# The gate's products in one stream of 512 columns, weights split on the vector engine, a reload in quarters and a new order of steps

## The chip, the core and the metric

The kernel runs on one core of a Trainium2 chip. The metric is device microseconds of that core; less is better. Engines are PE (matrix products), DVE (vector), ACT (scalar and activation), POOL (GpSimd) and SP, which issues most of the DMAs. Each works through its own instructions in order.

## What is computed

Three layers follow one another, all in fp32:

```
attention, 4 batches x 8 heads, 512 rows and 32 states each, width 64:
    a  = softmax(x @ state.T / 8)        xread = a @ state
    a2 = softmax(state @ x.T / 8)        sread = a2 @ x
    rows = concat(xread, sread) -> 4 * 544 = 2176 rows of 512
mixture of 8 experts: e = argmax(rows @ w_gate); the first 576 rows of
    an expert are kept; y = gate * (relu(row @ w1[e]) @ w2[e]), else 0
gated layer: out = (silu(y @ wg) * (y @ wv)) @ wo,   d_ff = 1536
```

## The kernel before

Batches of this input send all their 512 rows to one expert, and their 32 state rows to one expert. `one_expert_a_batch` builds on that, and a general path follows only where a register says that it isn't so. A matrix product in near fp32 precision is made of three products of split operands (hi and lo; `mm3`, L1464, run at L1466).

The work is cut into small steps, each a function under `@step`, named with batch b, half g or z (z = 0 the 512 rows, z = 1 the 32 state rows), block fc. An order written out by hand calls them, as `lg:1` or `up:0:3`; what an engine gets is in this order, and so is SP's queue of DMAs.

- Attention: `lx` (L1543) fetches a batch of x; `xt`, `xc` transpose it over PSUM; `sc` (L1611) makes scores, `sx` (ACT) copies them and `mx` (DVE) takes their maximum from the same PSUM bank; `tt`, `sub`, `ae`, `sn`, `an` and `ex2`, `et`, `ec`, `rs` are the two softmaxes; `rd`, `sr`, `qt`, `qc` read the states; `at`, `ah`, `al` turn the row softmax back and split it.
- Gate: the gate's matrix is folded with the states (`sg`, and `sgc` at L1586 splits it into `bsg`). `lg` (L1768) multiplies the rows' softmax with it, as 16 products with 8 or 16 moving columns each; `sl` does it for state rows. `ga`, `gb`, `gx` find the largest logit, `pq` (L1846) counts rows over partitions, `ge` writes the expert's number, `gf`, `gd`, `gp`, `gc` make gate weights. With a number known, `lu` (L1966) fetches w1 of this expert in four pieces of 512 KB, `ld` (L1979) w2 piece by piece, in eight shared buffers.
- Expert: `pj` (L1992) folds states and w1, `pa`, `pd` split it; for eight blocks `up`, `hh`, `hl`, then `wh`, `wl`, `dn`, with four PSUM banks for the result; `yt`, `yh`, `yl` (POOL) scale and split it. Batch 0 stays on the chip in `xb`; batches 1 and 2 go to DRAM (`ys`, tensor yd). `n1` to `n4` treat the narrow parts (state rows and the 64 kept rows of batch 3), gathered in `yF`.
- Gated layer, first block of 512 rows: w2l (L2191) fetches 36 pieces of weights, 64-bit words, in four buffers `raw2`; `da` (ACT, L2203), `db` (three DVE steps, L2212, L2213, L2216), `dc` (ACT, L2234) turn a piece into fp32 hi, and `dd` (POOL, L2239) makes lo; two tiles `hv` take part. `fu` (24 products), `fs`, `fm`, `fh`, `fl`, `fd` (12) compute a block fc as soon as its weights are there.
- Then, all weights on the chip, blocks of 512, 448 and 256 rows (`block`): rows of batch 1 are read back from yd into `xc` (`load_set`, L2466) in two DMAs of 1 MB, in the place that `raw2` gave up; `finish` copies results out of PSUM, and `rows_of`, `rest_rows` store them.

Of the kernel before, what the change touches and what calls it, by code (L numbers as in the profile page):

```python
# [1395 lines left out]
def one_expert_a_batch(  # L1396
# [890 lines left out]
    with tc.manual_schedule():  # L2287
        run("""
            lx:0 lx:1 st:0 stc:0 xt:0:0 xc:0:0 xc:0:2 st:1 xc:0:1 xc:0:3 stc:1 sc:0 sg:0 mx:0:0
            sx:0:0 sx:0:1 mx:0:1 tt:0:0 ex2:0:0 tt:0:1 sub:0:0 sg:1 ex2:0:1 xt:1:0 sub:0:1  # L2290
# [4 lines left out]
            et:1:1 sl:0 ec:1:1 ge:0:0 ae:1:1 rd:1 ga:0:1 lu:0:0 gb:0:1 gx:0:1 sr:1 sn:1:0 pq:0:1
            qt:1 qc:1 ge:0:1 sl:1 an:1:0 sn:1:1 lu:0:1 at:1:0 ah:1:0 ga:1:1 an:1:1 gf:0:0 gx:1:1
            at:1:1 al:1:0 gd:0:0 ah:1:1 pj:0:0 gf:0:1 ld:0:0:0 al:1:1 gd:0:1 ld:0:1:0 pa:0:0:0
            lg:1 ld:0:0:1 pa:0:0:1 pd:0:0:0 pd:0:0:1 pj:0:1 ga:1:0 gb:1:0 gx:1:0 gb:1:1 pa:0:1:0
            pq:1:0 up:0:0 pa:0:1:1 ge:1:0 gf:1:0 gp:0:0 hh:0:0 gp:0:1 gc:0:0 pd:0:1:0 gd:1:0
            gc:0:1 pd:0:1:1 n1:0:1 hl:0:0 wh:0:0 wh:0:1 wl:0:0 pq:1:1 lu:1:0 n1a:0:1 gp:1:0  # L2300
# [219 lines left out]
```

## Time and profile before

| | |
|---|---|
| three timed runs | 583.09 us median (582.48 to 584.33) |
| profiled execution | 584.99 us, span of the trace 583.3 us |
| busy share of the span | PE 94%, PE weight loads 76%, DVE 47%, ACT 33%, POOL 14% |
| mean granted clock of PE | 0.953 of 2.4 GHz |
| DMA | 72.51 MB, mean 124 GB/s |

An instruction's time in the trace runs from its start to its end; those of PE are pipelined, so that two starts are closer than one takes. A releaser behind an arrow is what ended the idle time before a row. A clock between the two levels (1.2 and 2.4 GHz) in a stretch is a mean over it.

### The profile page before, as it was taken

How to read it: one execution, taken by the hardware profiler on the slowest of the kernel's cores; microseconds unless marked ns; L12 is line 12 of the kernel's file. 1: busy time of each engine (PE TensorE's matmuls, PEld its weight loads, DVE VectorE, ACT ScalarE, POOL GpSimd, SP SyncE). 2: the span in 40 equal slices, each digit the busy share in tenths (PEclk: the TensorE clock that was granted, in tenths of full speed). 3: DMA queues.
4: the chain of work that ended last, by engine and by line, in shares of the span. 5: the costliest groups of instructions: out<-in, count | busy, mean ns of one | idle time of the engine just before them, and what ended most of it. 6: DMA issues, size and time to landing. Idle time of an engine off the chain costs nothing.

```text
span 583.3 us, 8745 instructions
## 1 busy us (share of the span) xinstructions
PE 547.0 (94%) x3418; PEld 444.0 (76%) x3418; DVE 271.9 (47%) x568; ACT 190.3 (33%) x367; POOL 81.5 (14%) x86
## 2 busy tenths in 40 slices
PE   4889999999789999999898799999999999999994
PEld 2676778886557778788676578888889888889993
DVE  1777327733863887799999311111121111122121
ACT  1643336433542553554555211111111111122111
POOL 1120001401300244334343100000000000000000
PEclk9966999899769999999999989999999999999998
DMA  7039997001796995758652630000040000001001
GB/s 146 18 119 360 280 278 264 2 1 72 242 364 197 376 338 180 253 157 261 189 178 75 231 131 0 1 0 1 0 136 9 1 0 1 1 30 34 2 1 42
DMA packets 66195, 72.51 MB, mean 124 GB/s; under 512 B 20384, under 2 KB 51872, under 8 KB 65632
## 3 DMA queue, kind: packets, MB, share of 16 engines
q1 hardware_dynamic: 62864, 70.98, 37.9%
q10 hardware_dynamic: 3280, 0.87, 0.8%
q8 instruction: 29, 0.48, 0.3%
q14 instruction: 22, 0.18, 0.1%
HBM read 62.14 MB, written 9.70 MB: 123 GB/s over the span
## 4 chain that ended last, share of the span: by engine, by line
PE 71%; DVE 10%; issue 6%; DMA 5%; POOL 4%; ACT 2%; ACTq 0%; SPq 0%; POOLq 0%; DVEq 0%
PE m L1466 45%; PE py L1466 13%; DVE hv L2213 3%; POOL w2r L2241 2%; PE m L1775 2%; PE m L1999 2%; DMA xcl<-yd 2%; PE m L2101 2%; POOL w L2241 1%; DMA yd<-y 1%; DMA xs<-in_x_dram 1%; PE m L1599 1%; PE m L1615 1%; DVE hv L2212 1%; PE py L2429 1%
## 5 line engine op out<-in xcount | busy, mean ns | idle before, releaser
L2417 DVE TENSOR_TENSOR sg<-sg,m 128x512 f32<-128x512 f32 (+2 forms) x36 | 20.8, 577 | 168.7 <-PE m L1466 168.7
L1466 PE MATMUL m<-xbh,w 128*128 128x512 f32 (+1 forms) x288 | 88.1, 377 | 0.6 <-POOL w L2241 0.6
L1466 PE MATMUL m<-xch,w 128*128 128x512 f32 (+1 forms) x288 | 74.3, 341 | 2.4 <-issue 2.4
L1466 PEld LDWEIGHTS m<-xbh,w 128*128 128x128 f32 x288 | 54.0, 188 | 8.9 <-POOL w L2241 1.0
L1466 PEld LDWEIGHTS m<-xch,w 128*128 128x128 f32 x288 | 50.9, 193 | 9.0 <-issue 2.8
L2416 ACT ACTIVATE sg<-m 128x512 f32<-128x512 f32 (+2 forms) x36 | 18.3, 509 | 112.2 <-PE m L1466 112.2
L1466 PE MATMUL m<-xbl,w 128*128 128x512 f32 (+1 forms) x144 | 54.3, 377 | 0.0
L1466 PE MATMUL m<-xcl,w 128*128 128x512 f32 (+1 forms) x144 | 49.5, 344 | 2.4 <-DMA xcl<-yd 2.4
L1474 ACT CAST hh<-sg 128x512 fp32r<-128x512 f32 (+2 forms) x36 | 19.1, 531 | 85.2 <-DVE sg L2417 85.2
L2241 POOL TENSOR_TENSOR w<-hv,w 128x512 fp32r<-128x512 f32 x26 | 36.9, 1418 | 67.6 <-ACT w L2236 67.6
L1466 PE MATMUL py<-w,hh 128*128 128x512 f32 x144 | 44.6, 391 | 0.0
L2213 DVE SCALAR_TENSOR_TENSOR hv<-raw,hv 128x512 int32<-128x512 int32 x36 | 43.4, 1205 | 1.2
L1466 PE MATMUL m<-hl,wh 128*128 128x512 f32 x96 | 38.9, 405 | 1.6 <-DVE hl L2030 1.6
L1466 PE MATMUL m<-hh,wh 128*128 128x512 f32 x96 | 39.7, 414 | 0.6 <-ACT hh L2025 0.6
L2216 DVE SCALAR_TENSOR_TENSOR hv<-hv 128x512 int32<-128x512 int32 x36 | 36.6, 1016 | 4.2 <-ACT hv L2206 0.7
L1466 PE MATMUL m<-hh,wl 128*128 128x512 f32 x96 | 38.5, 401 | 0.0
L1466 PE MATMUL m<-ah,wp 128*128 128x512 f32 x96 | 35.8, 414 | 0.0
L2206 ACT ACTIVATE hv<-raw 128x512 f32<-128x512 f32 x36 | 24.5, 680 | 31.3 <-POOL w L2241 19.4
L1466 PEld LDWEIGHTS m<-xcl,w 128*128 128x128 f32 x144 | 27.9, 194 | 6.2 <-DMA xcl<-yd 2.8
L1475 DVE TENSOR_TENSOR hl<-sg,hh 128x512 fp32r<-128x512 f32 (+2 forms) x36 | 20.9, 581 | 21.5 <-ACT hh L1474 21.5
L2042 DVE TENSOR_TENSOR wl<-rawb,wh 128x512 fp32r<-128x512 f32 x24 | 16.5, 690 | 30.1 <-ACT wh L2037 30.1
L1466 PEld LDWEIGHTS py<-w,hh 128*128 128x128 f32 x144 | 26.5, 188 | 4.9
(215 smaller groups left out, 974.9 us busy)
## 6 DMA issues: line engine op xcount, KB each, us to landing
rawa<-in_moe_w_dram SPq DMA_DIRECT2D x32, 512.0 KB, 6.4
rawb<-in_moe_w_dram SPq DMA_DIRECT2D x32, 512.0 KB, 7.4
raw<-in_moe_w_gate_dram SPq DMA_DIRECT2D x12, 512.0 KB, 6.0
raw<-in_moe_w_val_dram SPq DMA_DIRECT2D x12, 512.0 KB, 4.5
raw<-in_moe_w_out_dram SPq DMA_DIRECT2D x12, 512.0 KB, 4.7
yd<-y SPq DMA_DIRECT2D x8, 512.0 KB, 3.4
xs<-in_x_dram SPq DMA_DIRECT2D x14, 256.0 KB, 5.9
out_dram<-ot SPq DMA_DIRECT2D x11, 256.0 KB, 5.5
```

The source lines that it names most:

```text
L1466: nc.tensor.matmul(po, lh[a], rh[b], start=first and n == 0, stop=last_ and n == 2, tile_position=at)
L1474: nc.scalar.copy(hi, src)
L1475: nc.vector.tensor_tensor(lo, src, hi.bitcast(F32), op=ALU.subtract)
L1775: nc.tensor.matmul(po[:, c, 0:w].rearrange("p j e -> p (j e)"), v[b][part][g][:, s], bsg[:, 2 * b + g, 0:w].rearrange("p j e -> p (j e)"), ...
L1999: nc.tensor.matmul(pw[g][NS * k:NS * (k + 1), 256 * i:256 * (i + 1)], sT[r, b, NS * k:NS * (k + 1)], raws[b, 0][1][2 * h + i][r, k], start ...
L2042: nc.vector.tensor_tensor(w[1], raws[b, 0][2][fc // 2][:, fc % 2], w[0].bitcast(F32), op=ALU.subtract)
L2206: nc.scalar.activation(t[:, 0], Wn[fc, m][0][:, :, 1].bitcast(F32), AF.Copy, scale=2.0 ** -112)
L2213: nc.vector.scalar_tensor_tensor(vi, r[:, :, 0], 29, vi, op0=ALU.logical_shift_right, op1=ALU.bitwise_or)
L2216: nc.vector.scalar_tensor_tensor(vi, hw.bitcast(I32), 3, vi, op0=ALU.logical_shift_left, op1=ALU.bitwise_or)
L2241: nc.gpsimd.tensor_tensor(lo, Wn[fc, m][1][:, 1], hi.bitcast(F32), op=ALU.subtract)
L2416: nc.scalar.activation(sg, ph[0][:, 0:n], AF.Silu)
L2417: nc.vector.tensor_tensor(sg, sg, ph[1][:, 0:n], op=ALU.mult)
```

## The change

The softmax's rows are now the moving operand of `lg`: the folded gate's products, all four batches side by side in 128 columns, are held, and four products of 512 columns give logits, hi and lo part, by row of a [128, 512] bank. ACT copies it (`lc`), and four small fp32 products (`lt`) with `add2`, which picks a batch and adds its hi and lo rows, turn it back. `dd` moves from POOL to DVE. The rows of batch 1 come back through four DMAs of 512 KB into `raw2` buffers (`xc2`), from within the first block. `gF` has the tail ahead of the state rows, so that the last stores are four instead of six, and the last bank is copied in two halves. All of the order is new.

```
-    bsg = ctile([P, B * 2, 2, E], "bsg", F32R)
+    GQ = P // B
+    bsg = [ctile([P, B, GQ], "bsg%d" % g, F32R) for g in range(2)]
+    add2 = ctile([P, B, E], "add2")
+    for t in bsg:
+        nc.gpsimd.memset(t.bitcast(F32), 0.0)
...
     def sgc(g):
-        hi, lo = bsg[:, g::2, 0], bsg[:, g::2, 1]
+        hi, lo = bsg[g][:, :, 0:E], bsg[g][:, :, E:2 * E]
...
+        if g == 0:
+            i4 = ident.rearrange("p (b q) -> p b q", b=B)
+            nc.vector.tensor_tensor(add2, i4[:, :, 0:E], i4[:, :, E:2 * E], op=ALU.add)
...
     def lg(b):
-        v[b]["lg"] = po = bank([P, NC, 2, E], b == 0)
+        v[b]["lgs"] = po = bank([P, S], b == 0)
+        todo = [(g, part) for g in range(2) for part in ("hi", "lo")]
+        for g, part in todo:
+            nc.tensor.matmul(
+                po, bsg[g].rearrange("p b q -> p (b q)"), v[b][part][g],
+                start=(g, part) == todo[0], stop=(g, part) == todo[-1],
+            )
+    def lc(b):
+        v[b]["lgr"] = r = wk.tile([P, S], F32, tag="lgr", name="lgr")
+        nc.scalar.copy(r, v[b]["lgs"])
+    def lt(b):
+        v[b]["lg"] = po = bank([P, NC, E], b == 0)
         for c in range(NC):
-            s = slice(c * P, (c + 1) * P)
-            for n, (part, g) in enumerate((("hi", 0), ("lo", 0), ("lo", 1), ("hi", 1))):
-                w = 2 if part == "hi" else 1
-                nc.tensor.matmul(
-                    po[:, c, 0:w].rearrange("p j e -> p (j e)"), v[b][part][g][:, s],
-                    bsg[:, 2 * b + g, 0:w].rearrange("p j e -> p (j e)"),
-                    start=n == 0, stop=n == 3,
-                )
+            nc.tensor.matmul(
+                po[:, c], v[b]["lgr"][:, c * P:(c + 1) * P], add2[:, b], start=True, stop=True
+            )
...
     def ga(b, z):
-            src = small(z, "lsum")
-            nc.vector.tensor_reduce(
-                src, v[b]["lg"].rearrange("p c j e -> p c e j"), axis=AX.X, op=ALU.add
-            )
+        src = v[b]["pl" if z else "lg"]
...
     def dd(fc, m):
-        nc.gpsimd.tensor_tensor(lo, Wn[fc, m][1][:, 1], hi.bitcast(F32), op=ALU.subtract)
+        nc.vector.tensor_tensor(lo, Wn[fc, m][1][:, 1], hi.bitcast(F32), op=ALU.subtract)
...
+    def xc2(k):
+        t = raw2.tile([P, 2, 512], F32R, tag="raw", name="xc")
+        xc.append(t)
+        nc.sync.dma_start(t.bitcast(F32), yd[0, :, :, 512 * k:512 * (k + 1)])
...
     def finish(py, n, stores):
+            elif n < 512 and not half and j == len(py) - 1:
+                nc.scalar.copy(o[:, 0:256], p[:, 0:256])
+                nc.vector.tensor_copy(o[:, 256:DM], p[:, 256:DM])
...
     def rest_rows(j, t):
             nc.sync.dma_start(o[NC - 1, 64:P], t[0:64])
-            nc.scalar.dma_start(s_rows(0), t[64:64 + NS])
-            nc.scalar.dma_start(s_rows(1), t[64 + NS:P])
+            nc.scalar.dma_start(out[last * SEQ:last * SEQ + TAIL], t[64:P])
         else:
-            nc.sync.dma_start(out[last * SEQ:last * SEQ + TAIL], t[64:P])
-            nc.scalar.dma_start(s_rows(2), t[0:NS])
-            nc.sync.dma_start(s_rows(3), t[NS:64])
+            o = out.rearrange("(b s) d -> b s d", b=B)[:, S:SEQ]
+            for b in range(0, B, 2):
+                (nc.scalar if b else nc.sync).dma_start(o[b:b + 2], t[NS * b:NS * (b + 2)])
...
-    load_set(1, yd[0], 512)
     finish(fv["py"], S, rows_of(0))
```

Of the order, the places that matter here (each list is one engine-wide order; steps between are left out at "..."):

```
 first scores
- xc:0:1 xc:0:3 stc:1 sc:0 sg:0 mx:0:0 sx:0:0 sx:0:1 mx:0:1 tt:0:0
+ xc:0:1 xc:0:3 xt:1:2 stc:1 sc:0 sg:1 sx:0:0 mx:0:1 sx:0:1 mx:0:0 ex2:0:1 tt:0:1
 first expert
- lg:0 ex2:1:0 ... rd:0 ga:0:0 gb:0:0 ... pq:0:0 qc:0 ... ge:0:0 ... lu:0:0
+ rd:0 xc:1:1 ae:0:0 at:0:1 lx:2 ... lg:0 ... lc:0 ... lt:0 ... xt:2:0 ec:1:1 ga:0:0 xt:2:1 gb:0:0 ae:1:0 rd:1
+ xc:2:0 xc:2:1 gb:0:1 pq:0:0 ... ge:0:0 pq:0:1 ... lu:0:0
- pj:0:0 ... lg:1 ... pj:0:1 ga:1:0 ... up:0:0
+ pj:0:0 ... pj:0:1 ... lg:1 ... sl:1 lc:1 lt:1 ga:1:1 up:0:0 ... up:0:1
 batch 2 and the end of expert 0
+ pj:1:1 ... at:2:1 ... at:2:0 ... dn:0:6 ... lg:2 wh:1:0 lx:3 ... up:1:0 lc:2 rd:2 ... ld:0:1:3 ... lt:2 ... dn:0:7
+ ga:2:0 gb:2:0 gx:2:0 pq:2:0 ... n3:0:1 yt:0:0 yt:0:1 ... yt:0:2 ... dn:1:0 ... n1:1:1 ... lu:2:0
 batch 3
- dn:1:7 n1:1:1 yt:1:0 ... sc:3 ... tt:3:0 ... at:3:0 ... pj:2:0 ... lg:3 ... pj:2:1 ... up:2:0 ... dn:2:0
+ sc:3 ... dn:1:2 sx:3:0 mx:3:0 ... tt:3:1 ... up:1:3 ... up:1:4 ... pj:2:0 ... dn:1:3 ... at:3:1 ... pj:2:1 ...
+ al:3:0 ... dn:1:7 ... tx wh:2:0 yt:1:1 lg:3 ... up:2:0 ... lc:3 up:2:1 ... lt:3 ... yt:1:3 ... dn:2:0
 opening of the decoding buffers
- ... wh:2:2 gf:3:1 verdict up:2:1 ... up:2:2 gc:3:1 | ... w2l:0:0
+ ... wh:2:4 n2:2:1 dn:2:3 gc:3:1 | wl:2:4 n2a:2:1 w2l:0:0
 a block of weights
- da:4:1 w2l:5:1 dc:4:0 db:4:1 dd:4:0 n2:3:1 fd:2 n2a:3:1 da:4:2 fm:3 w2l:5:2 dc:4:1 db:4:2 fh:3 dd:4:1
+ db:4:0 da:4:1 db:4:1 w2l:5:1 dc:4:0 fu:3:1 dd:4:0 w2l:5:2 dc:4:1 ld:3:1:0 fl:2 ld:3:1:1 dd:4:1 fs:3
 its end
- da:11:2 fu:11:0 fm:10 dc:11:1 db:11:2 fh:10 dd:11:1 fu:11:1 fl:10 dc:11:2 fs:11 dd:11:2 fd:10
+ db:11:1 da:11:2 fd:9 fm:10 xc2:2 dc:11:1 db:11:2 fh:10 fu:11:0 dd:11:1 xc2:3 dc:11:2 fl:10 dd:11:2
+ fu:11:1 fs:11 fd:10 fm:11 fh:11 fl:11 fd:11
```

## Rows read from the trace of the kernel before

**Rows 1.** The page's first part: busy us, share of the span, instructions.

```profile
PE 547.0 (94%) x3418; PEld 444.0 (76%) x3418; DVE 271.9 (47%) x568; ACT 190.3 (33%) x367; POOL 81.5 (14%) x86
```

**Rows 2.** Busy time by stretches: length, engines (instructions), granted clock, DMA share, GB/s.

```profile
40.00:60.00 20.00, 19.05 (x146) 12.71 (x147) 14.51 (x65) 7.36 (x17) 3.87 (x6) 0.66 1.05 349
60.00:140.00 80.00, 79.93 (x561) 64.07 (x559) 39.09 (x82) 33.53 (x65) 8.43 (x8) 0.98 0.47 143
140.00:160.00 20.00, 16.18 (x231) 9.96 (x234) 14.62 (x44) 9.92 (x26) 7.17 (x7) 0.82 0.67 221
160.00:180.00 20.00, 17.82 (x146) 12.18 (x146) 11.09 (x50) 8.06 (x19) 0.28 (x1) 0.67 0.81 282
...
200.00:240.00 40.00, 40.00 (x220) 30.63 (x222) 30.61 (x48) 18.95 (x34) 16.07 (x11) 1.00 0.80 278
...
260.00:280.00 20.00, 18.59 (x85) 15.02 (x82) 19.17 (x25) 10.12 (x18) 9.88 (x7) 1.00 0.84 256
280.00:300.00 20.00, 18.55 (x80) 14.38 (x78) 19.07 (x24) 10.11 (x16) 8.33 (x7) 1.00 0.58 178
300.00:320.00 20.00, 18.11 (x75) 13.75 (x76) 19.17 (x24) 10.59 (x18) 8.41 (x7) 1.00 0.37 107
```

**Rows 3.** The chain that ended last: start us, us, what.

```profile
113.01 27.32 PE m L1466 x120
```

**Rows 4.** Timeline from 0 to 37 us, and one stretch by its busy times (columns as in rows 2).

```profile
14.27 1.96 PE L1615 MATMUL m<-xt,f_sT 64*32 64x512 f32 x16
...
17.71 1.97 PE L1638 MATMUL m<-f_ident,stt 128*128 128x128 f32 x8 [1.07 <-ACT stt L1625]
...
31.08 1.94 PE L1704 MATMUL m<-xs,e2t 128*32 128x64 f32 x64
...
36.93 8.18 SPq L1973 DMA_DIRECT2D rawa<-in_moe_w_dram  x8
...
16.00:17.00 1.00, 0.64 (x40) 0.54 (x28) 0.65 (x1) 0.00 (x0) 0.00 (x0) 1.00 0.06 11
```

**Rows 5.** Timeline at 17 us: copies of the first scores.

```profile
17.07 1.07 ACT L1625 COPY stt<-m 128x512 f32<-128x512 f32 x2 [4.83 <-DVE mx L1630]
```

**Rows 6.** Timeline: the counts' product, and the gate's products of batch 3.

```profile
34.92 0.45 PE L1848 MATMUL m<-f_cc,f_ones 128*128 128x16 f32 x2
...
163.40 3.58 PE L1775 MATMUL m<-f_bsg,part 128*128 128x16 f32 x16
```

**Rows 7.** Decoding: groups by shape; L2212 in one stretch; timeline from 262 us.

```profile
L2213 DVE SCALAR_TENSOR_TENSOR hv<-raw,hv 128x512 int32<-128x512 int32 x36 | 43.4, 1205 | 1.2
L2216 DVE SCALAR_TENSOR_TENSOR hv<-hv 128x512 int32<-128x512 int32 x36 | 36.6, 1016 | 4.2 <-ACT hv L2206 0.7
...
300.00:320.00 20.00, 2.51 (x6) 1.00 0.37 107
...
262.51 1.33 POOL L2241 TENSOR_TENSOR w<-hv,w 128x512 fp32r<-128x512 f32 x1 [1.30 <-ACT w L2236]
262.73 1.67 DVE L2213 SCALAR_TENSOR_TENSOR hv<-raw,hv 128x512 int32<-128x512 int32 x1
264.50 0.69 DVE L2216 SCALAR_TENSOR_TENSOR hv<-hv 128x512 int32<-128x512 int32 x1
```

**Rows 8.** Timeline of PE around the reload of batch 1's rows.

```profile
329.73 0.39 PE L1466 MATMUL m<-w2y,hl 128*128 128x512 f32 x1
332.48 1.15 PE L1466 MATMUL m<-xch,w 128*128 128x512 f32 x4 [2.36 <-issue]
336.04 0.80 PE L1466 MATMUL m<-xcl,w 128*128 128x512 f32 x1 [2.41 <-DMA xcl<-yd]
...
340.75 0.40 PE L1466 MATMUL m<-xcl,w 128*128 128x512 f32 x1
```

**Rows 9.** Timeline of the end: last copy and last store.

```profile
575.23 0.69 DVE L2397 COPY ot<-py 128x512 f32<-128x512 f32 x1 [1.38 <-PE py L1466]
...
576.75 0.57 SPq L2464 DMA_DIRECT2D out_dram<-ot  x1
```

More of the change, by code (lines that the diff above doesn't have):

```diff
@@ L2279, in fd @@
             mm3(fv["py"][j], [a[:, c] for a in h], W2[fc, 2], fc == 0, fc == NF - 1)
+    xc = []
+    @step
+    def xc2(k):
+        t = raw2.tile([P, 2, 512], F32R, tag="raw", name="xc")
+        xc.append(t)
+        nc.sync.dma_start(t.bitcast(F32), yd[0, :, :, 512 * k:512 * (k + 1)])
     def run(text):
@@ L2295, in one_expert_a_batch @@
[L2295 to L2300, printed above, removed]
@@ new lines, in one_expert_a_batch @@
+            dn:0:0 gf:1:0 gf:1:1 gd:1:0 hl:0:1 gd:1:1 gp:1:0 ld:1:0:0 wh:0:2 up:0:2 lu:0:1
+            gc:1:0 wl:0:2 sc:2 hh:0:2 hl:0:2 gp:1:1 dn:0:1 sx:2:0 mx:2:1 sx:2:1 mx:2:0 ex2:2:1
+            gc:1:1 ex2:2:0 up:0:3 wh:0:3 rs:2 wl:0:3 pj:1:0 hh:0:3 hl:0:3 tt:2:1 ld:0:1:0
+            pa:1:0:0 tt:2:0 ld:0:1:1 pa:1:0:1 sub:2:1 dn:0:2 ld:0:0:3 pd:1:0:0 ae:2:1 pd:1:0:1
+            sn:2:1 up:0:4 wh:0:4 wl:0:4 an:2:1 n1:0:1 hh:0:4 sub:2:0 hl:0:4 ae:2:0 dn:0:3
+            n1a:0:1 sn:2:0 an:2:0 up:0:5 wh:0:5 wl:0:5 n2:0:1 hh:0:5 et:2:1 n2a:0:1 dn:0:4
@@ new lines, in one_expert_a_batch @@
+            ae:3:0 pj:2:0 hl:1:3 hh:1:4 sn:3:1 dn:1:3 pa:2:0:0 pa:2:0:1 hl:1:4 an:3:1 sn:3:0
+            up:1:5 wh:1:5 pd:2:0:1 an:3:0 wl:1:5 dn:1:4 hh:1:5 pd:2:0:0 hl:1:5 up:1:6 wh:1:6
+            wl:1:6 dn:1:5 hh:1:6 hl:1:6 up:1:7 wh:1:7 wl:1:7 n3:1:1 hh:1:7 hl:1:7 at:3:1 lu:2:1
+            n3a:1:1 pj:2:1 axa:1 axv:1 ah:3:1 at:3:0 pa:2:1:1 al:3:1 dn:1:6 ah:3:0 axv:0
+            pd:2:1:1 axa:0 pa:2:1:0 ld:2:1:0 al:3:0 ld:2:0:2 pd:2:1:0 ld:2:1:1 dn:1:7 wh:2:1
+            ld:2:1:2 ld:2:1:3 wl:2:1 tx wh:2:0 yt:1:1 lg:3 txc yt:1:0 yh:1:1 up:2:0 wl:2:0
@@ new lines, in one_expert_a_batch @@
+            yh:1:0 yl:1:1 lc:3 up:2:1 hh:2:0 yl:1:0 yt:1:2 hl:2:0 lt:3 hh:2:1 ys:1:0 yt:1:3
+            n4:1:1 et:3:1 ys:1:1 ga:3:0 dn:2:0 gb:3:0 gx:3:0 ec:3:1 hl:2:1 n4v:1:1 yh:1:2 pq:3:0
+            yh:1:3 rd:3 yl:1:2 ge:3:0 n4a:1:1 gf:3:0 dn:2:1 yl:1:3 sr:3 ys:1:2 n4l:1:1 gd:3:0
+            ys:1:3 gp:3:0 wh:2:2 qt:3 up:2:2 gc:3:0 wl:2:2 qc:3 wh:2:3 sl:3 hh:2:2 wl:2:3 up:2:3
+            ga:3:1 gb:3:1 gx:3:1 silu n1:2:1 hl:2:2 hh:2:3 hl:2:3 pq:3:1 n1a:2:1 dn:2:2 ge:3:1
+            gf:3:1 verdict gd:3:1 gp:3:1 wh:2:4 n2:2:1 dn:2:3 gc:3:1
@@ L2351, in one_expert_a_batch @@
+            fs:0 db:1:2 da:2:0 n1:3:0 yt:2:0 w2l:3:0 dc:1:2 yt:2:1 ld:3:0:3 yh:2:0 db:2:0 yh:2:1
+            yl:2:0 yl:2:1 fu:0:1 n1a:3:0 yt:2:2 w2l:3:1 dc:2:0 yv:2:0 yt:2:3 yv:2:1 dd:1:2
+            n2:3:0 fm:0 da:2:1 fu:1:0 dd:2:0 n2a:3:0 fh:0 db:2:1 da:2:2 n3:3:0 db:2:2 w2l:3:2
+            dc:2:1 ys:2:0 ys:2:1 dd:2:1 fl:0 da:3:0 fu:1:1 fs:1 db:3:0 yh:2:3 yh:2:2 yl:2:3
+            n3a:3:0 yl:2:2 yv:2:3 n4:3:0 fd:0 fm:1 n4v:3:0 fh:1 yv:2:2 ys:2:2 n4a:3:0 fl:1
+            ys:2:3
         """)
@@ L2380, in one_expert_a_batch @@
     tc.no_sync_barrier()
-    exr.close()
-    xtc = ctx.enter_context(tc.tile_pool(name="f_xtc", bufs=1, side="right"))
-    sets = [xb, [xtc.tile([P, KD, 512], F32R, name="xc" + c) for c in "hl"]]
+    sets = [[[a[:, k] for k in range(KD)] for a in xb], [[a[:, q] for a in xc] for q in range(2)]]
     def finish(py, n, stores):
@@ L2452, in rest_rows @@
     def rest_rows(j, t):
-        def s_rows(b):
-            return out[b * SEQ + S:(b + 1) * SEQ]
         if j == 0:
@@ L2458, in rest_rows @@
             nc.sync.dma_start(o[NC - 1, 64:P], t[0:64])
-            nc.scalar.dma_start(s_rows(0), t[64:64 + NS])
-            nc.scalar.dma_start(s_rows(1), t[64 + NS:P])
-        else:
-            nc.sync.dma_start(out[last * SEQ:last * SEQ + TAIL], t[64:P])
-            nc.scalar.dma_start(s_rows(2), t[0:NS])
-            nc.sync.dma_start(s_rows(3), t[NS:64])
+            nc.scalar.dma_start(out[last * SEQ:last * SEQ + TAIL], t[64:P])
+        else:
+            o = out.rearrange("(b s) d -> b s d", b=B)[:, S:SEQ]
+            for b in range(0, B, 2):
+                (nc.scalar if b else nc.sync).dma_start(o[b:b + 2], t[NS * b:NS * (b + 2)])
     def load_set(i, src, n):
+        if i:
+            for k in range(KD):
+                nc.sync.dma_start(
+                    xc[k].bitcast(F32)[:, :, 0:n],
+                    src.rearrange("p q (k n) -> p k q n", k=KD)[:, k, :, 0:n],
+                )
+            return
         for q in range(2):
             nc.sync.dma_start(
-                sets[i][q].bitcast(F32)[:, :, 0:n],
+                xb[q].bitcast(F32)[:, :, 0:n],
                 src[:, q].rearrange("p (k n) -> p k n", k=KD)[:, :, 0:n],
             )
-    load_set(1, yd[0], 512)
     finish(fv["py"], S, rows_of(0))
```

135 lines of the change are left out of this document (58 added, 77 removed).

## The prediction

> **What bounds the kernel now.** The page comes first: the matmul engine (PE) is busy for 94% of the span [rows 1], so time can only go where PE waits, or where it works at a low clock. The table by stretches says where that is [rows 2]. From 60 to 140 us and from 200 to 240 us PE has nearly no gap at a granted clock of 0.98 to 1.00; that is PE's own work, and the change takes next to none of it away. Back to back, 120 products of 512 columns took 27.32 us, 0.228 us each [rows 3]; that is the 2.4 GHz level, and at 1.2 GHz the same product takes twice as long.
>
> Four places lose time. In 40 to 60 us the clock is 0.66. In 140 to 180 us PE is idle for 3.82 and 2.18 us, and the means of 0.82 and 0.67 lie between the two levels: 20 x 0.18 + 20 x 0.33 = 10.2 us of full-speed work were not done; together 16.2 us [rows 2]. From 260 to 320 us the clock is full, yet PE is idle for 1.41 + 1.45 + 1.89 = 4.75 us while the vector engine (DVE) is busy for 57.4 of 60 us: there DVE, which decodes the gated layer's weights, is the bound [rows 2]. Around 330 us PE stands still for a reload.
>
> The profiled run took 584.99 us, of which 583.3 are its span; the median of the three timed runs is 583.09. I add the terms to 584.99 and take the 1.90 us of difference off at the end.
>
> **The first 60 us: +4.7 us here, -1.7 later.** The new list puts the transposes of batch 1 (xt:1:2) ahead of the first scores (sc:0). PE works in order, so sc:0, which began at 14.27 us [rows 4], now waits for the whole of batch 1's x, which the same queue brings last; its data come in until a little after 16 us (the DMA engines' share is down to 0.06 in 16 to 17 us) [rows 4]. Four transposes more, and sc:0 starts near 16.8 us: +2.5. Against it, sx:0:0 now stands beside mx:0:1: in the trace the ACT copy waited for the DVE maximum over the same bank [rows 5], and with the swap each engine has its own: -0.7. Further on pq:0:0, whose counts choose the first expert, stands on PE behind xt:2:0, xt:2:1 and rd:1. Eight transposes took 1.97 us here [rows 4], rd took 1.94 [rows 4]; of these 3.9 us the ten small DVE steps of ga and gb cover some 2 us: +2. The x of batch 2 is now fetched ahead of the first expert's weights; were it late, pq:0:0 would wait for it too: +0.9 as an estimate, between 0 and 3. Sum +4.7: the weights' fetch, at 36.93 us before [rows 4], leaves nearer 41.5. The bounds are 0 and +8, the lower one if everything is covered. The eight transposes are then missing from the dense stretch later, about 1.7 us with what waits for them.
>
> **The gate's products (lg, lc, lt): 0.** Before, 16 products took 3.58 us [rows 6] at the low clock. Now four of 512 columns take 4 x 0.228 at the full level and 1.8 us at the low one; lc, a copy of 128x512 on ACT, is half of the 1.07 us pair in the trace [rows 5], 0.53. The four turning products in fp32 are bounded by the counts' product pq, one such product in two instructions: 0.45 us at the low clock [rows 6], so up to 1.8 us, and 0.6 if they pipeline. I take 1.2, since four in a row share fill and drain. That is 3.5 against 3.58; the small reduction over two halves goes as well. With four batches the bounds are -4 and +3 us, most of it under other work. The two memsets on POOL and the sum add2 on DVE stand ahead of everything that waits; if that cover went, they would cost under 1 us. The narrow columns moved in gF cost nothing.
>
> **Batches 2 and 3 inside the experts: -12 us.** Before, scores, softmax and gate of batch 3 stood after the last down-projection of expert 1, with nothing else for PE; that is the stretch of 140 to 180 us. In the new list sc:3 to al:3 lie among up:1:3 to dn:1:7, and pj:2 (expert 2's folded weights) is done before expert 1 ends, so lg:3 and lt:3 are followed by up:2:0, up:2:1 and dn:2:0. The 16.2 us lose their cause. I leave 4.2 us of them: dn:1:0 needs all four yt of expert 0, which on DVE stand among the gate's small steps of batch 2; n3:0:1 needs a weight piece behind the 1 MB of lx:3 on SP's queue; and the four yt of expert 1 alternate with POOL over two buffers ahead of dn:2:0. SP's ld and lu are issued in the list's new order; lu:2:0 stands behind n1:1:1, which frees its buffers, and has dn:1:2, up:1:3 and up:1:4 as cover before pj:2:0, 24 products or 5.5 us. Bounds: -16.2 and -6.
>
> **The weights' split on DVE: -3.6 us.** A weight costs DVE three steps (db) today; the middle and last take 1.205 and 1.016 us on average, where a step of that shape without POOL beside it takes 0.69 [rows 7]. In single rows: a POOL split started at 262.51 and ran 1.33 us; the DVE step at 262.73 took 1.67 us, the next one, after POOL's end, 0.69 [rows 7]. So POOL's split holds DVE up. With dd on DVE a weight gains 0.515 + 0.326 and pays 0.69: -0.15 us; six weights fall into 20 us [rows 7], so 24 into the dense 80 us: -3.6, at most the 4.75 us that PE is idle. DVE is still the bound: the three weights of a block cost 3 x (0.42 + 3 x 0.69) + 2 x 0.69 = 8.9 us, PE's 36 products 8.2. Decoding starts later in PE's work than before (after dn:2:3, not up:2:2: some 8 us less to hide behind); I charge nothing, since DVE had 9.4 us idle in 200 to 240 us [rows 2]; without that cover it would be +4. So the bounds are -4.75 and +4.
>
> By the Trainium skill ("Perfetto Trace Analysis", Optimizing Scalar/DVE Operations) GpSimd and the vector engine share a read port, so moving work between the two might not help. By that this term would be 0 and the forecast 3.6 us later; the rows above say that the step of DVE gets back more than it pays, and they decide.
>
> **The reload in quarters: -6.9 us.** PE's last product of block one starts at 329.73 us; the next four start at 332.48, then PE waits 2.41 us for xcl<-yd, restarts at the low clock and is back at full level about 340.75 us [rows 8]. Those 11 us hold 15 products, 3.4 us at full level: 7.4 us lost. The loads could leave only at 325 us, once all decoding buffers were free. Now each quarter goes into one decoding buffer as it falls free, the fourth after db:11:2. PE then still has fu:11:1, fd:10 and fd:11, 36 products or 8.2 us, against some 5 us for 512 KB. I leave 0.5 us. Bounds -7.4 and -3, if the fourth is late.
>
> **The last rows: -0.5 us.** The last copy ended at 575.92 us, and the last of six stores was issued at 576.75, behind others of its queue [rows 9]; with four stores, one of each queue left after the copy, that is about 576.2. The copy of the last bank (0.69 us [rows 9]) is cut into halves on ACT and DVE, which would save another 0.3 us if they ran side by side. The Trainium skill ("PSUM — Partial Sum Buffer", PSUM bank collisions) keeps two engines off one bank at once; by it the halves run in turn and save nothing. The row agrees: ACT's copy waited for DVE on one bank [rows 5]. Bounds -1 and +0.3.
>
> **Sum.** 4.7 - 1.7 + 0 - 12 - 3.6 - 6.9 - 0.5 = -20.0; 584.99 - 20.0 = 565.0 us for a profiled run, 563.1 against the median. I forecast 563.
>
> **Rivals.** First, *half the middle stays* and the start is worse: PE in order only moves its waits from 140 us to dn:1:0, dn:2:0 and the first experts. It keeps 8 instead of 4.2 us, the start costs 8 instead of 4.7, DVE gives nothing: 563 + 3.8 + 3.3 + 3.6 = 574. For it speaks that the clock is low through 40 to 60 us, where any delay costs double; against it the dense 60 to 140 us, where batch 2 is already mixed in without loss. Chance 0.18.
>
> Second, *more comes out*: the start costs nothing net, the whole 16.2 us go, PE never waits for DVE: 563 - 3 - 4.2 - 1.2 = 555. Chance 0.13.
>
> Third, *the quarters don't do what they say*: the last one waits behind DVE's splits, and PE stands as long as before: 563 + 6.9 = 570. Chance 0.05.
>
> Fourth, **slower**: the split in DVE's queue waits for ACT's cast of the same weight, with only two decoding tiles to work on. If the long steps stay at 1.205 and 1.016 us and each split adds 0.69 and a cast's wait of 0.6 us, a weight costs 1.3 us more than today's 3.3; over 24 weights that is +31 where I count -3.6: 563 + 3.6 + 31 = 598. It decides once a weight takes 0.7 us more than today (16.4 us of other gains over 24 weights). Against it: the new list puts another weight's db, fm or fl between a cast and its split, and the long steps go with POOL's. Chance 0.06.
>
> **How the numbers follow.** My forecast has 0.58, the rivals 0.18, 0.13, 0.05 and 0.06. The predicted time is that of the likeliest. The range of 552 to 576 takes in the two rivals that are faster, the 574 and the ends of the large terms, and leaves out the slower case. A change of 0.3%, 1.7 us, is about what a measurement of this kernel can tell from none. Only the fourth rival ends above; a sum of bad bounds could land at no change. So faster 0.92, same 0.02, slower 0.06.
>
> **What would show it.** Right: PE's gap at the reload is gone and 1.00 stands through that slice; 140 to 180 us have no low clock; POOL is nearly idle after the experts, and L2213 and L2216 of before have a mean of 0.69 us; PE's first folded product (pj) starts later than 43 us. Wrong: long steps of DVE without POOL; gaps before each DVE split; a low clock after 60 us; a fourth quarter that lands after PE's last fd.

## The result, and the profile after

The changed kernel takes 565.58 us (median of four runs, 564.59 to 566.53), the kernel before, run beside it, 582.79; the ratio is 0.971 with an interval of 0.966 to 0.975. The forecast was 563.0 in a range of 552 to 576. The profiled execution takes 566.21 us with a span of 564.6, at a mean granted clock of 0.981.

The first part of the page, and the table by stretches (length, then busy time of PE, weight loads, DVE, ACT and POOL, then clock, DMA share, GB/s), of the changed kernel:

```profile
PE 528.6 (94%) x3402; PEld 430.4 (76%) x3402; DVE 263.3 (47%) x601; ACT 193.2 (34%) x372; POOL 31.7 (6%) x52
```

```profile
40.00:60.00 20.00, 14.23 (x112) 9.82 (x112) 11.94 (x47) 7.16 (x16) 2.82 (x4) 0.74 0.53 184
60.00:140.00 80.00, 78.79 (x643) 58.77 (x643) 48.99 (x135) 38.01 (x78) 12.62 (x12) 1.00 0.77 242
140.00:160.00 20.00, 20.00 (x181) 15.65 (x179) 10.92 (x19) 9.85 (x21) 2.55 (x2) 1.00 0.55 184
160.00:180.00 20.00, 20.00 (x182) 14.89 (x181) 11.99 (x52) 8.57 (x22) 3.05 (x4) 1.00 0.38 133
200.00:240.00 40.00, 36.99 (x219) 27.05 (x217) 29.77 (x55) 17.63 (x31) 5.53 (x4) 1.00 0.82 255
260.00:280.00 20.00, 20.00 (x145) 16.37 (x144) 19.01 (x35) 11.43 (x20) 0.00 (x0) 1.00 0.71 228
280.00:300.00 20.00, 20.00 (x90) 16.57 (x89) 18.93 (x34) 12.08 (x20) 0.00 (x0) 1.00 0.67 211
300.00:320.00 20.00, 20.00 (x90) 16.58 (x89) 8.76 (x14) 5.08 (x9) 0.00 (x0) 1.00 0.64 219
```

Against [rows 2], 140 to 180 us are now full at the full clock, and so are 260 to 320 us. New is a loss of 3.0 us between 200 and 240 us, where there was none; and 40 to 60 us are no better: PE is idle for 5.77 us there at a mean clock of 0.74, where it was idle for 0.95 us at 0.66.

The reload, in the timeline of PE (against [rows 8]): the second block follows 0.22 us behind the last fd and runs on at full clock.

```profile
313.48 0.39 PE L1466 MATMUL m<-w2y,hl 128*128 128x512 f32 x1
313.70 11.04 PE L1466 MATMUL m<-xc,w 128*128 128x512 f32 x48
```

The end, in the timeline: last product, copies, last issues (against [rows 9]).

```profile
551.14 0.40 PE L1466 MATMUL py<-w2y,hl 128*128 128x512 f32 x1
551.49 0.56 ACTq L2481 DMA_DIRECT2D out_dram<-ot  x1
552.10 0.37 ACT L2418 COPY ot<-py 128x256 f32<-128x256 f32 x1 [0.64 <-PE py L1466]
552.50 0.42 DVE L2419 COPY ot<-py 128x256 f32<-128x256 f32 x1 [2.33 <-ACT ot L2418]
552.96 0.63 SPq L2485 DMA_DIRECT2D out_dram<-ot  x1
552.96 1.34 ACTq L2485 DMA_DIRECT2D out_dram<-ot  x1
```

PE's last product moved from 574.80 to 551.14 us, by 23.7. The end of the span moved by only 18.8 us: from the last product to the end there were 8.5 us, and now there are 13.4.

To compare the two orders, in which work changes its place, I count every PE instruction of a stretch at the pitch that its shape has in dense rows at full clock (0.2275 us for a product of 512 columns, 0.11 us for one of 8 or 16), and call what is left of the stretch lost. This is an estimate.

| | forecast us | lost time, after less before |
|---|---|---|
| first 60 us, net of the 1.7 us that come back later | +3.0 | +1.4 |
| 60 to 180 us, batches 2 and 3 | -12 | -14.3 |
| 180 to 320 us, decoding | -3.6 | -3.4 |
| reload | -6.9 | -7.3 |
| behind PE's last product | -0.5 | +4.9 |
| PE's own work (gate's products) | 0 | 0 |
| sum | -20.0 | -18.7 |

The first row is no larger than the scatter: five kernels that are the same up to 60 us (they are named in the last section) lie between -1.3 and +2.2 us by this count.

### The profile page after: what moved, and what is told of

The parts are those of the page before. It is cut to its first block, busy times and chain, and to the rows that moved or that the text cites. A ratio compares the mean times of both kernels' runs of the same rounds, so it can differ in the third digit from the quotient of the medians.

```text
span 564.6 us, 8671 instructions
## 1 busy us (share of the span) xinstructions
PE 528.6 (94%) x3402; PEld 430.4 (76%) x3402; DVE 263.3 (47%) x601; ACT 193.2 (34%) x372; POOL 31.7 (6%) x52
## 4 chain that ended last, share of the span: by engine, by line
PE 80%; DVE 7%; DMA 5%; ACT 2%; issue 1%; SPq 1%; POOL 1%; ACTq 1%; POOLq 0%; DVEq 0%
PE m L1466 57%; PE py L1466 13%; DMA rawb<-in_moe_w_dram 2%; DVE hv L2227 1%; DMA yd<-y 1%; DMA f_wgt<-in_moe_w_gate_dram 1%; PE m L2151 1%; PE m L2115 1%; PE py L2453 1%; PE m L1624 1%; DMA rawa<-in_moe_w_dram 1%; DVE hv L2230 1%; DMA xs<-in_x_dram 1%; DVE w L2255 1%; DVE t L2071 1%
## 5 line engine op out<-in xcount | busy, mean ns | idle before, releaser
L1466 PE MATMUL m<-xc,w 128*128 128x512 f32 (+1 forms) x432 | 77.4, 336 | 0.0
L1466 PEld LDWEIGHTS m<-xc,w 128*128 128x128 f32 x432 | 67.5, 190 | 9.1
L2440 ACT ACTIVATE sg<-m 128x512 f32<-128x512 f32 (+2 forms) x36 | 18.3, 508 | 104.4 <-PE m L1466 104.4
L1474 ACT CAST hh<-sg 128x512 fp32r<-128x512 f32 (+2 forms) x36 | 19.1, 531 | 85.7 <-DVE sg L2441 85.7
L1466 PE MATMUL m<-hl,wh 128*128 128x512 f32 x96 | 37.5, 391 | 0.0
L1466 PEld LDWEIGHTS m<-xbl,w 128*128 128x128 f32 x144 | 27.1, 188 | 3.9
L1466 PE MATMUL py<-w,hl 128*128 128x512 f32 x72 | 28.1, 390 | 0.0
L2230 DVE SCALAR_TENSOR_TENSOR hv<-hv 128x512 int32<-128x512 int32 x36 | 25.8, 717 | 3.7
L2227 DVE SCALAR_TENSOR_TENSOR hv<-raw,hv 128x512 int32<-128x512 int32 x36 | 25.9, 719 | 1.2
L2250 ACT CAST w<-hv 128x512 fp32r<-128x512 f32 x26 | 16.1, 622 | 27.8 <-DVE hv L2230 22.0
```

The lines of the kernel that those rows point to most:

```text
L1466: nc.tensor.matmul(po, lh[a], rh[b], start=first and n == 0, stop=last_ and n == 2, tile_position=at)
L1474: nc.scalar.copy(hi, src)
L2227: nc.vector.scalar_tensor_tensor(vi, r[:, :, 0], 29, vi, op0=ALU.logical_shift_right, op1=ALU.bitwise_or)
L2230: nc.vector.scalar_tensor_tensor(vi, hw.bitcast(I32), 3, vi, op0=ALU.logical_shift_left, op1=ALU.bitwise_or)
L2250: nc.scalar.copy(t[:, 0], Wn[fc, m][1][:, 1])
L2440: nc.scalar.activation(sg, ph[0][:, 0:n], AF.Silu)
```

## The experiments

Each kernel is the changed one with the edit shown. The kernel before ran beside each set of four; its medians there were 581.64, 582.60 and 584.16 us, so that between sets 1 to 2 us mean little. Where that is so, the place in the trace decides.

**Stores by batch.**

```
-            for b in range(0, B, 2):
-                (nc.scalar if b else nc.sync).dma_start(o[b:b + 2], t[NS * b:NS * (b + 2)])
+            for b in range(B):
+                (nc.scalar if b % 2 else nc.sync).dma_start(o[b], t[NS * b:NS * (b + 1)])
```

> The changed kernel, but its last bank leaves in four stores of one batch (32 rows) each, two on each queue, instead of two stores of two batches each. Theory: a store over two batches is cut so that few of the DMA engines get its packets, and that is the 4.9 us by which the stretch from PE's last product to the end of the span grew (8.5 us before, 13.4 after). Then about 565.6 - 4.9 + 0.3 = 561.0 us, and the last packets land within some 2.5 us of the last issue. Rival: the copy in two halves, or the new order of the narrow columns, is what made the end longer; then 565 to 566 us, packets still thin after 554 us.

Measured: 563.56 us (ratio to before 0.967, 0.958 to 0.975). From the last product (554.20) to the end (span 562.6) are 8.4 us: the 5.0 us are back. The median shows only 2.0 of them; its profiled run lost time elsewhere, in 40 to 60 us (see the last section) and, 4.8 us by the count above, in 220 to 240 us, where the changed kernel lost 1.1. The DMA view of the end, from 548 to 564.5 us of the changed kernel (busy share of the engines in tenths by 40 slices, GB/s by the same slices, then packets, then the issues):

```profile
DMA  0000000010078801112212111110110000000000
GB/s 0 0 0 0 0 0 0 0 40 0 0 154 179 323 5 25 30 10 70 70 35 60 30 45 45 50 65 35 45 50 35 25 25 25 0 0 0 0 0 0
DMA packets 300, 0.61 MB, mean 37 GB/s; under 512 B 36, under 2 KB 36, under 8 KB 292
out_dram<-ot SPq DMA_DIRECT2D x2, 128.0 KB
out_dram<-ot ACTq DMA_DIRECT2D x2, 128.0 KB, 2.9
```

and from 551 to 562.5 us with stores by batch:

```profile
DMA  0000000000010000498949995000100001000000
DMA packets 360, 0.61 MB, mean 53 GB/s; under 512 B 96, under 2 KB 96, under 8 KB 352
out_dram<-ot SPq DMA_DIRECT2D x1, 128.0 KB
out_dram<-ot ACTq DMA_DIRECT2D x1, 128.0 KB, 2.9
out_dram<-ot SPq DMA_DIRECT2D x2, 64.0 KB
out_dram<-ot ACTq DMA_DIRECT2D x2, 64.0 KB
```

The bytes are the same. With stores by batch they leave mostly at 8 or 9 tenths of the engines; over two batches at 2 tenths or less, for nearly 8 us by the GB/s row. The packets under 512 B (4 bytes each) tell how a store was shared out: six stores have 96 of them, 16 each; the four stores of the changed kernel have 36, which is 2 x 16 for the first two and 2 for each of those over two batches. So, by this count, each of these ran on two of sixteen engines.

The Trainium skill says this ("DMA: Bandwidth & Descriptors", Why a DMA increments its semaphore by 16 and not by 1): a DMA is shared over the largest number of engines, up to 16, that divides the slowest dimension of both its sides. Here these are 64 partitions and 2 batches, which gives 2, and the trace agrees with its 36 packets.

**Undivided last copy.**

```
-            elif n < 512 and not half and j == len(py) - 1:
-                nc.scalar.copy(o[:, 0:256], p[:, 0:256])
-                nc.vector.tensor_copy(o[:, 256:DM], p[:, 256:DM])
```

> The changed kernel with its last bank copied whole by DVE, as before the change; the stores over two batches stay. If the stores are what is slow: 565.6 us within 0.5 (one copy of about 0.69 us for two halves of 0.37 and 0.42 us in turn). If the halves are the cause of the long end: 561. If the halves did save their 0.3 us somewhere: 565.9.

Measured: 564.88 us (0.972, 0.965 to 0.980). Just outside the first case: the end is 12.2 us instead of 13.4. In the timeline, with the last product at 547.95:

```profile
548.38 0.69 DVE L2418 COPY ot<-py 128x512 f32<-128x512 f32 x1 [1.40 <-PE py L1466]
549.10 0.63 SPq L2482 DMA_DIRECT2D out_dram<-ot  x1
```

The stores are issued 1.15 us behind the last product; with halves it was 1.82 (551.14 to 552.96). The halves cost 0.67 us for two reasons that the rows of the changed kernel show: they run in turn (552.10, 552.50), and ACT's half begins only when ACT's queue is done with issuing a store (551.49 + 0.56). The rest of the 1.2 us by which the end is shorter is not explained.

**Both edits of the end.**

> The changed kernel with both edits of its end: stores by batch, and the last bank copied whole by DVE. From PE's last product to the end of the span: 13.41 us in the changed kernel, 8.39 with the stores by batch alone, 12.23 with the undivided copy alone. If both effects are what the traces say, they add: 7.2 us, and 565.6 - 6.2 = 559.4 us. Rival: the undivided copy's 1.2 us is a matter of when the stores meet, and adds nothing here: 560.6. If neither holds and the ends only differed by chance: 564 to 566.

Measured: 561.15 us (0.964, 0.960 to 0.968). In the trace the end is 8.5 us (549.73 to 558.20), no shorter than with the stores alone. By this trace the rival holds, and the copy's gain does not add in the span. It is not settled: the two later kernels with the same end ("four edits together" and the last one) have 7.9 and 8.0 us there, so that up to 0.5 us of it may remain. The median is 4.4 us below the changed kernel's, of the 4.9 by which the end had grown.

**The split back on POOL.**

```
-        nc.vector.tensor_tensor(lo, Wn[fc, m][1][:, 1], hi.bitcast(F32), op=ALU.subtract)
+        nc.gpsimd.tensor_tensor(lo, Wn[fc, m][1][:, 1], hi.bitcast(F32), op=ALU.subtract)
```

> The changed kernel with one line back: the weights' lo part (dd) is computed on POOL again, in the new order. The forecast's step: the two long DVE steps of the decoding go from 0.72 us back toward 1.2 and 1.0, DVE is the bound from 240 to 310 us again, and the time is 565.6 + 3.6 = 569.2 us (567.5 to 571). Rival, that moving work between the two engines changes nothing here: 565.6 within 0.6. Second rival, that the new order leans on DVE's split (two decoding tiles, split late behind POOL): over 572.

Measured: 574.08 us (0.988, 0.980 to 0.995), 8.5 more; in the trace PE ends 5.4 us later. Groups of the page (number, busy us, mean ns), of the changed kernel and of this one:

```profile
L2230 DVE SCALAR_TENSOR_TENSOR hv<-hv 128x512 int32<-128x512 int32 x36 | 25.8, 717 | 3.7
L2227 DVE SCALAR_TENSOR_TENSOR hv<-raw,hv 128x512 int32<-128x512 int32 x36 | 25.9, 719 | 1.2
```

```profile
L2255 POOL TENSOR_TENSOR w<-hv,w 128x512 fp32r<-128x512 f32 x26 | 36.8, 1418 | 57.7 <-ACT w L2250 48.9
L2227 DVE SCALAR_TENSOR_TENSOR hv<-raw,hv 128x512 int32<-128x512 int32 x36 | 39.6, 1099 | 1.2
L2230 DVE SCALAR_TENSOR_TENSOR hv<-hv 128x512 int32<-128x512 int32 x36 | 36.4, 1010 | 3.9 <-ACT hv L2220 0.4
```

One line changes the two long steps by 0.38 and 0.29 us each, and in the same rows the split itself takes 1.42 us on POOL. The second rival, over 572 us, holds. By the trace, from the first fu to the last fd, the decoding takes 124.0 us instead of 117.7. In the new order DVE's split is worth more than the 3.6 us that I gave it against the old one. How much of this is the long steps and how much the late split with only two decoding tiles, this edit does not separate.

**The reload at once.** xc2 is taken out of the list; behind the decoding its buffers are given up, and two loads of 1 MB go into a tile of their own.

```
-        ... xc2:0 ... xc2:1 ... xc2:2 ... xc2:3
+    exr.close()
+    xtc = ctx.enter_context(tc.tile_pool(name="f_xtc", bufs=1, side="right"))
...
+    load_set(1, yd[0], 512)
     finish(fv["py"], S, rows_of(0))
```

> The changed kernel, but the rows of batch 1 come back as before the change: two loads of 1 MB into a tile of their own, in the place that the decoding buffers give up when all of them are free. Forecast's step: PE stands still and falls to the low clock between the last fd and the second block, 565.6 + 7 = 572.5 us (571 to 573.5). Rival: as the new list ends its decoding earlier, some 10 us before the last product, the two loads are hidden as well and the quarters are worth 0 to 2 us: 565.6 to 567.5.

Measured: 573.78 us (0.986, 0.979 to 0.994), 8.2 more. The gap of before stands there again, after a last fd at 314.00:

```profile
316.53 1.17 PE L1466 MATMUL m<-xch,w 128*128 128x512 f32 x4 [2.14 <-issue]
320.41 0.80 PE L1466 MATMUL m<-xcl,w 128*128 128x512 f32 x1 [2.71 <-DMA xcl<-yd]
```

From the last fd to the first output product of the second block are 19.1 us instead of 11.1. Decoding ended early here too: the last step that reads one of its buffers ran from 302.91 to 303.60 us. Yet the two loads were issued at 309.55 and 309.92 us, behind a load of the next rows (xbh) on SP's queue:

```profile
308.98 0.34 SPq L2493 DMA_DIRECT2D xbh<-yd  x1
309.55 0.33 SPq L2493 DMA_DIRECT2D xch<-yd  x1
```

That one overwrites what fu:11:1 still reads, whose last product starts at 308.56 us, so it could not leave before.

**Batch 3 behind expert 1.** The steps from sc:3 to al:3:0 move out of the blocks of expert 1 to right behind dn:1:7.

```
- ... dn:1:2 sx:3:0 mx:3:0 ... dn:1:6 ah:3:0 ... dn:1:7 wh:2:1
+ ... dn:1:7 sc:3 sx:3:0 mx:3:0 ... ah:3:0 axv:0 axa:0 al:3:0 wh:2:1
```

> The changed kernel, with the scores and both softmaxes of batch 3, from sc:3 to al:3, moved out of expert 1 to right behind its last down-projection (dn:1:7), in the same order. Expert 2's folded weights stay early. If the largest term of the forecast has the right cause (PE had nothing else while batch 3's softmax ran), PE stands and its clock falls between expert 1 and expert 2 again: 10 to 16 us lost, 576 to 582 us. Rival: it was the early folding of expert 2 and the spread over DVE, ACT and POOL that mattered, and the chain of batch 3 is covered by the rest: 565.6 to 569.

Measured: 581.35 us (0.997, 0.993 to 1.000): 15.8 more, all but the whole gain of the change. The stretches show the old picture, a PE without work and then a low clock:

```profile
140.00:160.00 20.00, 15.90 (x169) 11.49 (x167) 7.99 (x18) 7.01 (x14) 0.00 (x0) 1.00 0.54 186
160.00:180.00 20.00, 14.72 (x122) 11.32 (x123) 13.26 (x35) 9.88 (x23) 7.48 (x6) 0.74 0.17 62
```

So the early fold of expert 2 (kept here) does not bring the gain by itself; the place of batch 3's softmax does. Whether that place would bring it without the early fold was not tried.

**Scores first.**

```
- xc:0:1 xc:0:3 xt:1:2 stc:1 sc:0 sg:1
+ xc:0:1 xc:0:3 stc:1 sc:0 xt:1:2 sg:1
```

> The changed kernel, with the transposes of batch 1 (xt:1:2) behind the first scores again. In the changed kernel sc:0 starts at 16.00 us, after the last piece of x; here it should start at 14.3 as before the change. If this is on the path to the first weights, as the forecast's first term says, the fetch (lu:0:0, at 38.79) leaves some 1.5 us earlier and the time is about 564. Rival: the xt put off takes its place a few us later, on a PE and an ACT that are both busy, and the fetch leaves within 0.5 us of 38.8; then 565.6 within 1.

Measured: 563.35 us (0.968, 0.961 to 0.975), 2.2 less. sc:0 starts at 13.40, the counts pq:0:0 come at 33.55 instead of 36.86, the fetch leaves at 35.56 instead of 38.87, and dn:0:0 starts 2.1 us earlier.

**Fold before casts.**

```
- pd:0:0:0 wh:0:0 pd:0:0:1 wh:0:1 wl:0:0 wl:0:1 lg:1 pa:0:1:1 pa:0:1:0 pd:0:1:1 pd:0:1:0 sl:1 lc:1 lt:1
+ pd:0:0:0 pd:0:0:1 lg:1 pa:0:1:1 pa:0:1:0 pd:0:1:1 pd:0:1:0 sl:1 lc:1 wh:0:0 wh:0:1 wl:0:0 wl:0:1 lt:1
```

> The changed kernel, with the casts and splits of the first two w2 pieces (wh:0:0, wh:0:1, wl:0:0, wl:0:1) behind those of expert 0's second folded half (pa:0:1, pd:0:1) and the copy lc:1. In the changed kernel PE stands idle from 49.6 to 52.4 us: ACT's wh:0:0 waits for a w2 piece until 49.7, and pa:0:1 and lc:1, whose inputs lie ready at 48.2 and 49.3, are queued behind it; lt:1 and up:0:0 wait for them. Theory: up:0:0 starts near 52 instead of 54.1, and the time falls by 2 us, to 563.5 (562.5 to 564.5). Rival: the casts are then late for dn:0:0 (60.53), and it starts where it did: 565.6 within 1.

Measured: 565.42 us (0.972, 0.964 to 0.980): no change. The wait in the changed kernel, in ACT's timeline (three rows) and PE's:

```profile
49.71 1.14 ACT L2051 CAST wh<-rawb 128x512 fp32r<-128x512 f32 x2 [3.04 <-DMA rawb<-in_moe_w_dram]
50.75 1.06 ACT L2022 CAST wp<-m 128x512 fp32r<-128x512 f32 x2
51.71 0.60 ACT L1790 COPY lgr<-m 128x512 f32<-128x512 f32 x1
...
52.40 1.85 PE L1797 MATMUL m<-f_add,lgr 128*128 128x8 f32 x8 [2.75 <-ACT lgr L1790]
```

PE's wait before lt:1 went from 2.75 us to 0.20, as the theory said; but in this execution PE was at the low clock from 45 to 51 us (0.50, where the changed kernel shows 0.98), and up:0:0 started at 54.49 instead of 54.10. So what the wait itself is worth is not shown here.

**Stores of batch 2 first.**

```
- w2l:3:2 dc:2:1 ys:2:0 ys:2:1 dd:2:1
+ ys:2:0 ys:2:1 w2l:3:2 dc:2:1 dd:2:1
```

> The changed kernel, with the stores of batch 2's first two row groups (ys:2:0, ys:2:1) ahead of the weight piece w2l:3:2 on SP's queue instead of behind it. In the changed kernel PE waits from 217.6 to 220.6 us: ACT's yh:2:3 waits for these stores to free a buffer, n3a:3:0 is queued behind it on ACT, and PE's n4:3:0 waits for that. The rows were ready at 206 us, but SP stood at w2l:3:2, whose buffer came free at 211.05, and issued the stores at 211.48. Theory: the stores leave at 206, PE's gap of 3 us is gone, and the time falls by 2.5 to 4 us, to 562.5. Rival: DVE sets the pace of the decoding from there on, and what PE doesn't wait for here it waits for by 260 us: 565 to 566.

Measured: 563.20 us (0.967, 0.960 to 0.975), 2.4 less. The wait in the changed kernel, one row each of SP's, ACT's and PE's timeline:

```profile
211.48 1.19 SPq L2090 DMA_DIRECT2D yd<-y  x2
218.13 0.62 ACT L2081 CAST y<-t 128x512 fp32r<-128x512 f32 x1 [2.59 <-DMA yd<-y]
220.64 0.44 PE L2167 MATMUL m<-f_ident,ny 128*128 128x128 f32 x2 [2.98 <-ACT ny L2161]
```

and with the stores first:

```profile
206.11 1.19 SPq L2090 DMA_DIRECT2D yd<-y  x2
216.23 1.13 ACT L2081 CAST y<-t 128x512 fp32r<-128x512 f32 x2
218.29 0.38 PE L2167 MATMUL m<-f_ident,ny 128*128 128x128 f32 x2
```

The stores leave 5.4 us earlier, no row waits, and from the first fu to the last fd are 114.7 us instead of 117.7.

**Narrow products.** In lg the new operand gives way to the old one (bsn, four small casts on DVE), lc and lt leave the list:

```
+                    po[:, c, 0:w].rearrange("p j e -> p (j e)"), v[b][part][g][:, s],
+                    bsn[:, 2 * b + g, 0:w].rearrange("p j e -> p (j e)"),
```

> The changed kernel with the gate's products of before: 16 products with 8 or 16 moving columns for each batch, no copy (lc) and no turning products (lt), and the reduction over two halves again; four small casts on DVE fill the old operand. Forecast's step: the two forms cost the same, 565.6 within 1.5, and the counts of batch 0 (pq:0:0, at 36.86 us) come at 36 to 38. Rival: the stream of 512 columns is part of the gain, and the old products with their weight loads put PE back by some 3.6 us for each batch: 569 or more. Rival on the other side: the copy and the turn behind it make the counts late, and without them pq:0:0 comes 2 us earlier: 563.5.

Measured: 566.04 us (0.972, 0.968 to 0.976), the changed kernel's within 0.5. At the full clock the 16 products take 2.3 us (30.88 to 33.17), with a short wait in them, and pq:0:0 comes at 38.14, a little past the 36 to 38 expected; sc:0 was 0.7 us later already in this execution (16.67). The form of the gate's products is worth nothing by itself.

**Four edits together**: stores by batch, undivided copy, scores first, stores of batch 2 first.

> The changed kernel with the four edits that each took time away: stores by batch, undivided last copy, the first scores ahead of batch 1's transposes, and batch 2's first stores ahead of w2l:3:2. Theory: the terms lie in different stretches of PE's order and add: 565.6 - 5.0 - 1.2 - 2.1 - 2.4 = 554.9 us (553.5 to 556.5). Rival: an earlier start is lost again at the decoding, where DMA and DVE set the pace, and the stretch of 200 to 240 us takes what the head gives: 557 to 558.

Measured: 554.29 us (0.951, 0.947 to 0.955). The gains of head, decoding and end add: by the medians they are 2.2, 2.4 and 4.4 us (both edits of the end), 9.0 in sum, and the four together show 11.3, with sets 1 to 2 us apart.

**And the first block ahead of batch 1's gate**: on top of the four edits, the order of "fold before casts", and up:0:0 ahead of lt:1.

> The four edits, and the gate of batch 1 put behind the first block's products: pa:0:1, pd:0:1 and lc:1 ahead of the casts of w2 pieces, and up:0:0 ahead of lt:1. Theory: PE's wait of 1.6 to 2.8 us before lt:1 is gone, up:0:0 starts some 3 us earlier, and dn:0:0 follows 1 to 2 us earlier: 553.5. Rival: at the low clock PE has work all the time up to dn:0:0 anyway, or the casts come late for dn:0:0; then as without it, 555 within 1. Against: lu:1:0 leaves 3 us later, and pj:1:0 waits for it: 557.

Measured: 552.50 us (0.949, 0.945 to 0.953). In the trace up:0:0 starts at 46.36 (50.48 without) and dn:0:0 at 52.36 (56.24); PE ends 2.6 us earlier. The first row is the wait in the kernel of four edits, the second PE at the same place here:

```profile
49.59 1.03 PE L1797 MATMUL m<-f_add,lgr 128*128 128x8 f32 x8 [2.66 <-ACT lgr L1790]
```

```profile
46.36 0.50 PE L1466 MATMUL m<-ah,wp 128*128 128x512 f32 x1
```

By the two medians it is 1.8 us, and their intervals overlap: that it is faster than the four edits alone is likely, not shown. Both beat the changed kernel and the one before: 552.5 against 565.6 and 584.2.

## Why the prediction was right, and where it was not

**The cause and the size were right**: 563 was forecast and 565.6 measured; the sum was -20.0, the trace gives -18.7 by the table. That they agree so closely is in part luck: the end missed by 5.4 us to one side, and batches 2 and 3 and the first 60 us by 2.3 and 1.6 to the other.

**Last rows: this step failed** (-0.5 forecast, +4.9 measured). I took "four stores, one of each queue left after the copy" as the cost, which counts issues, and asked nothing about how a store drains. The stores by batch end 5.0 us sooner from the same rows. The bounds, -1 and +0.3, were far too narrow, because the nearest row that I took [rows 9] showed an issue and a copy, not a store with its dimensions in this order. On the copy the rule cited from the Trainium skill ("PSUM — Partial Sum Buffer", PSUM bank collisions) held: the halves ran in turn. That ACT's half would stand behind its own queue's issue I had not seen; undivided, the stores leave 0.67 us sooner, though beside stores by batch little or nothing of this showed in the span.

**Batches 2 and 3** (-12; -14.3): the mechanism was right, the size was off. I left 4.2 us of loss at dn:1:0, dn:2:0 and pj:2:0; from 140 to 180 us PE has no gap. By the count these 40 us lost 18.3 us before and lose 1.9 now, while 60 to 140 us lose 2.1 more than they did. The 16.2 that I read from the means was thus no bound, though it counts idle time at a low clock twice, by up to 1.4 us. Moving the chain back cost 15.8 us. The rival by which half of this stays falls.

**The split** (-3.6; -3.4): [rows 7] said that the long steps go when POOL's split goes, and they did (1.205 and 1.016 to 0.72 and 0.72). PE waits no more from 260 to 320 us. The rule from the Trainium skill ("Perfetto Trace Analysis", Optimizing Scalar/DVE Operations), that moving work between the two engines might not help, did not decide here: one line is worth 8.5 us. That the two share a port fits the trace, in which the same DVE steps take 1.10 and 1.01 us with the split on POOL and 0.72 without. The agreement of the sums hides two things. In the new order the split on DVE is worth 6.3 us of decoding, more than I gave, and a wait that I did not foresee takes 3.0: stores of batch 2 behind a weight fetch on SP's queue. I named for SP's queue ld, lu and lx, but not ys.

**The reload** (-6.9; -7.3, and 8.2 when taken back): right in size. The reason that I gave for the late loads, buffers not yet free, was wrong: with buffers free 6 us earlier they still stood behind xbh on SP's queue. The kernel before shows it too: its last step that reads a buffer ended at 322.5 us, xbh left at 324.71 and the loads at 325.27. The quarters gain because their issues stand ahead of it.

**The first 60 us** (+3.0 net; +1.4, within the scatter): the path was wrong in half. The fetch left at 38.87 us, 1.9 later than before [rows 4], where I had added 4.7, and PE's first folded product came at 43.58 instead of 43.11. The scores behind batch 1's transposes were 1.7 us later, where I said 2.5, and cost 2.1 to 2.2 us of time. The 2 us for pq:0:0 behind xt:2 and rd:1 did not come: in "scores first", with these still ahead of it, pq:0:0 comes at 33.55, sooner than the 34.92 of before [rows 6]. Instead PE waits 2.75 us for the copy lc:1. In the step on the gate's products I had put it "under other work"; it stands on ACT behind casts that wait for a DMA.

**The gate's products** (0; 0): right; narrow products give the same time.

## What to carry to other kernels

Ask of each store not only when it is issued but over how many DMA engines it is shared: merging stores saved two issues and cost 5 us, and the count of 4-byte packets in the DMA view tells it at once. When work is spread into another's stretch, walk through each queue for what stands behind a buffer that comes free late: here a store behind a weight fetch on SP, and a copy behind a cast on ACT, were waits of 2 to 3 us each; one edit of the order gave the first back, and what the second is worth was not settled. And compare stage by stage: a total near the forecast held one term off by 5 us and others by 2.
